# Short groups of small matrix products joined, and k turned by VectorE and DRAM for six units, in an HGRN2 + SwiGLU kernel

## The chip, the cores and the metric

The kernel runs on one core of a Trainium2 chip. The metric is the device time of one execution in microseconds (us). A core has engines that each work through their own instructions in order and wait for one another through semaphores: TensorE (PE, matrix products; PEld is its loading of weights), VectorE (DVE), ScalarE (ACT), GpSimd (POOL) and SyncE (SP, which here issues most of the transfers). SBUF is the on-chip memory with 128 partitions; PSUM is the memory that TensorE writes, in eight banks of 128 x 512 float32; DRAM lies outside the core.

## What is computed

Two blocks follow each other. The first is a linear attention with a gate, for 4 batches, 8 heads, 768 steps and heads 48 wide; the second is a SwiGLU layer on 3072 tokens of width 384, with a hidden width of 1536.

```python
f = 1.0 / (1.0 + np.exp(-f_logit))
for t in range(S):                       # S = 768, state is (B, H, 48, 48)
    state = f[:, :, t, :, None] * state + np.einsum('bhd,bhe->bhde', k[:, :, t], v[:, :, t])
    y[:, :, t] = np.einsum('bhd,bhde->bhe', q[:, :, t], state)
x = y.transpose(0, 2, 1, 3).reshape(B * S, H * D)
g = x @ w_gate
out = (g * (1 / (1 + np.exp(-g))) * (x @ w_val)) @ w_out
```

## The kernel before

The sequence is cut into 6 chunks of 128 steps. A *unit* is one batch b in one chunk c; units are numbered u = 4c + b, so there are 24. `attention(u)` (L527) is a generator: each `yield` ends a step, and the caller decides when the next one is written into the program. A unit's steps for c >= 2 (`SQUARES` = 2, L315), in their order:

- sigmoid of f on ScalarE (L541), transposes of f and k in 32 x 32 squares on VectorE (L547, L554), a backward scan of the gates (`tails`, L558), four tiny operations, k times tails (`kT`, L568: the decayed k), a forward scan (`head`, L571), the transpose of q (L574, after which `load_after` issues the next unit's loads), q times head (`qT`, L577), the state times the chunk's whole decay (`decayed`, L581);
- **scores**: 8 products kT by qT on TensorE into two PSUM banks (`sc`, L595); then four 128 x 128 transposes of kT on TensorE (L599), because the sum for the state needs k with time on the partitions (`kt`, copied to SBUF by ScalarE, L603);
- the causal mask of the scores on VectorE (`A`, two operations, L605), which empties the score banks;
- **output**: products of qT with the decayed state and of A with v (`y`, L623 and L627; for the last batch L648 with a block-diagonal state, whose buffer GpSimd clears, L585), two copies by ScalarE and ten small transfers that put y into `xT`;
- **the state's sum**: 8 products kt by v (`dS`, L668), added to `decayed` by VectorE (L675).

TensorE counts each float32 product twice in the profile: 8 products are x16 there, and 2 are x4.

Block c of the SwiGLU layer (`mlp_fifteen`, L848) takes the tokens of chunk c and runs while the units of chunk c+1 are worked on. `token_sums` (L856) forms sums of token tiles. Then come four *triples* (L883) of 15 products each (L896, PSUM tags A: 2 banks, B: 1, o: 2, and c, which shares the o banks; L1183). ScalarE copies the results out (L901: `aside` has three buffers), VectorE combines them (L795, L798), ScalarE applies SiLU (L912), VectorE multiplies (L846) into the hidden tiles `h`. After the triples `down_seven` (L976) runs 14 half pieces of the product with w_out (L999, L1062): one, six, two, three, four, five, seven. `hidden_sums` (L987) and two more rounds of differences prepare `h` for them, tile by tile.

The order of all this is written out by hand. A planner counts time in its own units (`PRODUCT` = 0.86 for one product, `DOWN` = 3.9 for one piece, L782) and writes a unit's next step into the program when its count reaches the due time in `UNITS_2` or `UNITS` (L785 to L789; `come_in`, L1201). VectorE operations handed to `lag` (L845) are written one piece later. At the end `in_order` (L1229) fixes the order of PE, DVE and ACT as written; POOL and SP are ordered by the scheduler. For each unit three times matter here: the scores, the output, and the state's sum right after the output. So TensorE leaves its large products twice per unit: once for scores and transposes, once for output and state's sum. PSUM banks for scores, y, kt and dS come from `bank` (L515), three banks in this stage.

At the very end each engine reads a flag (`values_load`, L1267) and branches past a slower path that is not taken here.

Of the kernel before, what the change touches and what calls it, by code (L numbers as in the profile page):

```python
# [9 lines left out]
FP32 = mybir.dt.float32  # L10
# [279 lines left out]
def short_path(ctx, tc, ident, least, judge, q, k, v, f_logit, moe_w_gate, moe_w_val, moe_w_out, out):  # L290
# [29 lines left out]
    ffn = ctx.enter_context(tc.tile_pool(name="ffn", bufs=2))  # L320
    sums_pool = ctx.enter_context(tc.tile_pool(name="sums", bufs=1))
# [205 lines left out]
    def attention(u):  # L527
# [4 lines left out]

        def transposed(name, src):
# [17 lines left out]
        qT = att.tile([128, HP, C], FP32, tag="qT", name="qT")  # L551
# [18 lines left out]
        head = att.tile([128, n], FP32, tag="head", name="head", bufs=1)  # L570
        nc.vector.tensor_tensor_scan(head, gate[:, 0:n], start, 1.0, op0=ALU.mult, op1=ALU.add)  # L571
# [5 lines left out]
        nc.vector.tensor_tensor(qT, qp, pairs(head)[:, :, 1:N1], ALU.mult)  # L577
        if 0 < c < SQUARES:
            load_after(u)
        if c:  # L580
            nc.vector.tensor_tensor(decayed[:, :, 0:D], states[b], whole.broadcast_to((128, HP, D)), ALU.mult)  # L581
        if c and b == B - 1:

            diagonal = att.tile([128, HP, 2 * D], FP32, tag="x", name="diagonal")
            nc.gpsimd.memset(diagonal, 0.0)  # L585
            for par in range(2):
                nc.scalar.copy(diagonal[rows_of(par), :, par * D:(par + 1) * D], decayed[rows_of(par), :, 0:D])
# [3 lines left out]
        sc = [bank("sc") for _ in range(2)]  # L591
# [4 lines left out]
        if c < NCH - 1:  # L596
            p = bank("kt")
            for a in range(HP):
                nc.tensor.transpose(p[:, a * C:(a + 1) * C], kT[:, a, :], ident)  # L599
        yield  # L600
        if c < NCH - 1:
            kt = att.tile([128, H, W], FP32, tag="kt", name="kt")
            nc.scalar.copy(kt, p.rearrange("t (h d) -> t h d", d=W))  # L603
        for par in range(2):
            nc.vector.tensor_tensor(A[:, par], sc[par].rearrange("p (a t) -> p a t", t=C),  # L605
                                    causal.unsqueeze(1).broadcast_to((128, HP, C)), ALU.mult)
        yield
# [57 lines left out]
        if c < NCH - 1:  # L665
            p = bank("dS")
            for h in range(H):
                nc.tensor.matmul(p[W * (h % 2):W * (h % 2) + W, (h // 2) * D:(h // 2 + 1) * D],  # L668
                                 lhsT=kt[:, h, :], rhs=v_[:, h, 0:D], start=True, stop=True)
            dS = p[:, 0:HP * D].rearrange("p (a d) -> p a d", d=D)  # L670
        yield
# [6 lines left out]
    def load_after(u):  # L678

        w = u + (1 if units[u][1] >= SQUARES else 2)  # L680
        if w < len(units) and (units[w][1] >= SQUARES) == (w == u + 1):
            load(w)

    def attention_steps(c):

        runs = [attention(c * B + b) for b in range(B)]
        parts = [3, 5, 2, 3]
# [23 lines left out]
    def hidden_tile():  # L711

        return ffn.tile([128, 4, TH], FP32, tag="h", name="h", bufs=NP)

    def mlp_plain(c):
# [9 lines left out]
        def part(j):  # L725
            if j % NP not in h:
                h[j % NP] = hidden_tile()
# [578 lines left out]
```

## Time and profile before

| | |
|---|---|
| median of 15 runs | 616.38 us (615.61 to 617.98) |
| the profiled execution | 616.81 us, its span 615.1 us |
| granted TensorE clock, mean | 0.996 of full speed |
| chunks 0 and 1 with the plain first block, 0 to 148 us | PE busy 140.1, DVE 130.4, ACT 63.5 us |
| block 2, 244.3 to 340.4 us (96.1) | PE 95.8, DVE 80.4, ACT 48.9 us |
| block 3, 340.4 to 436.5 us (96.1) | PE 95.8, DVE 80.4, ACT 48.9 us |
| block 4 with chunk 5, 436.5 to 529.4 us (92.9) | PE 92.4, DVE 73.3, ACT 44.8 us |
| block 5 without attention, 529.4 to 615.1 us (85.7) | PE 79.6, DVE 46.9, ACT 33.9 us |

Busy time is summed from the instructions' records on each engine. A matrix product's record overlaps the next one's, so the step from start to start is the better measure of what a product costs; the timeline gives starts. "Idle before, releaser" names how long an engine stood still before an instruction and who ended that wait.

### The profile page before, as it was taken

Reading aid. Unit: us, or ns where it says so; the run is one execution under the profiler, and the core shown is the slowest. Engines: PE = TensorE matmul, PEld = TensorE weight load, DVE = VectorE, ACT = ScalarE, POOL = GpSimd, SP = SyncE. Lnnn points to the kernel's source line nnn. Section 1 sums busy time; section 2 is a strip of 40 time slices with the busy share of each in tenths; the row PEclk is TensorE's granted clock in tenths of the full one; section 3 lists DMA queues with packets and bytes.
Section 4 is the critical chain, followed back from the end, with each engine's and each line's share of the span. In section 5 each row is a group of like instructions: output and inputs, shape, how many; then the busy total and the mean of one; then the engine's idle time right before and its main releaser. Section 6 shows DMA issues by size and latency. Waiting matters only on the chain.

```text
span 615.1 us, 10901 instructions
## 1 busy us (share of the span) xinstructions
PE 599.6 (97%) x4060; PEld 491.0 (80%) x4060; DVE 500.7 (81%) x961; ACT 291.4 (47%) x534; POOL 5.0 (1%) x27
## 2 busy tenths in 40 slices
PE   7799999999999999999999999999999999999996
PEld 4654545666888899888899888899988889988895
DVE  7899989878999988968997886987887985566741
ACT  2465645312766721557722567642267640366600
POOL 1000000000000000000000000000000000000000
PEclk9999999999999999999999999999999999999999
DMA  9999582005222334222124420323331300100001
GB/s 150 245 214 280 172 248 78 3 12 157 81 72 52 78 78 116 79 50 59 46 66 116 117 53 17 86 61 96 102 80 35 82 5 10 53 2 0 1 2 56
DMA packets 95679, 50.95 MB, mean 83 GB/s; under 512 B 56065, under 2 KB 89473, under 8 KB 95617
## 3 DMA queue, kind: packets, MB, share of 16 engines
q1 hardware_dynamic: 93600, 47.41, 31.5%
q10 hardware_dynamic: 2016, 2.75, 1.2%
q8 instruction: 34, 0.56, 0.4%
q14 instruction: 29, 0.23, 0.1%
HBM read 42.47 MB, written 4.72 MB: 77 GB/s over the span
## 4 chain that ended last, share of the span: by engine, by line
PE 93%; ACT 2%; DVE 1%; DMA 1%; issue 1%; ACTq 0%; DVEq 0%
PE o L999 19%; PE A L896 17%; PE B L896 13%; PE o L896 6%; PE gate L721 5%; PE o L746 5%; PE c L896 5%; PE val L721 5%; PE sc L595 4%; PE o L1062 3%; PE y L627 2%; PE y L648 2%; PE kt L599 2%; PE dS L668 2%; PE y L623 1%; DMA fraw<-in_f_logit_dram 1%
## 5 line engine op out<-in xcount | busy, mean ns | idle before, releaser
L896 PE MATMUL A<-xs,w_both 128*128 128x256 f32 x240 | 62.1, 381 | 1.1 <-ACT aside L901 1.1
L999 PE MATMUL o<-w_out,h 128*128 128x192 f32 x360 | 62.1, 327 | 0.2 <-ACT aside L901 0.2
L999 PEld LDWEIGHTS o<-w_out,h 128*128 128x128 f32 x360 | 58.6, 190 | 0.8 <-ACT aside L901 0.4
L795 DVE TENSOR_TENSOR c<-c,aside 128x512 f32<-128x512 f32 x60 | 41.0, 684 | 13.7 <-ACT aside L901 12.6
L896 PEld LDWEIGHTS A<-xs,w_both 128*128 128x128 f32 x240 | 44.8, 190 | 8.7 <-ACT aside L901 2.8
L901 ACT COPY c<-A 128x512 f32<-128x512 f32 x40 | 23.3, 583 | 58.2 <-PE A L896 51.2
L901 ACT COPY aside<-A 128x512 f32<-128x512 f32 x60 | 35.0, 583 | 33.6 <-PE A L896 33.6
L798 DVE TENSOR_TENSOR c<-c,aside 128x512 f32<-128x512 f32 x60 | 41.0, 684 | 7.3 <-ACT aside L901 7.3
L846 DVE TENSOR_TENSOR h<-h,c 128x256 f32<-128x256 f32 x100 | 41.0, 418 | 7.0 <-ACT h L912 6.7
L999 PE MATMUL o<-ws,h 128*128 128x192 f32 x240 | 41.7, 328 | 0.0
L896 PE MATMUL B<-xT,extra 128*128 128x256 f32 x160 | 41.4, 381 | 0.0
L896 PE MATMUL A<-xs,extra 128*128 128x256 f32 x160 | 41.2, 380 | 0.0
L896 PE MATMUL c<-xT,w_both 128*128 128x256 f32 x160 | 41.2, 380 | 0.0
L896 PE MATMUL B<-xs,w_both 128*128 128x256 f32 x160 | 41.1, 379 | 0.0
L912 ACT ACTIVATE h<-c 128x256 f32<-128x256 f32 x100 | 39.2, 415 | 2.8 <-DVE c L798 1.7
L901 ACT COPY aside<-B 128x512 f32<-128x512 f32 x60 | 34.9, 582 | 10.2 <-PE B L896 10.1
L999 PEld LDWEIGHTS o<-ws,h 128*128 128x128 f32 x240 | 39.2, 190 | 0.3 <-issue 0.2
L798 DVE TENSOR_TENSOR c<-o,c 128x512 f32<-128x512 f32 x40 | 27.4, 686 | 12.3 <-ACT h L912 9.5
L605 DVE TENSOR_TENSOR A<-sc,causal 128x512 f32<-128x512 f32 x48 | 30.6, 677 | 5.2 <-PE sc L595 5.2
L896 PEld LDWEIGHTS B<-xs,w_both 128*128 128x128 f32 x160 | 30.4, 190 | 4.1
L896 PEld LDWEIGHTS A<-xs,extra 128*128 128x128 f32 x160 | 30.3, 190 | 4.2
L896 PEld LDWEIGHTS c<-xT,w_both 128*128 128x128 f32 x160 | 30.3, 190 | 4.2
(135 smaller groups left out, 1154.2 us busy)
## 6 DMA issues: line engine op xcount, KB each, us to landing
fsquares<-in_f_logit_dram SPq DMA_DIRECT2D x64, 96.0 KB, 2.3
ksquares<-in_k_dram SPq DMA_DIRECT2D x64, 96.0 KB, 2.3
qsquares<-in_q_dram SPq DMA_DIRECT2D x64, 96.0 KB, 2.3
v<-in_v_dram SPq DMA_DIRECT2D x24, 192.0 KB, 3.5
w<-in_moe_w_gate_dram SPq DMA_DIRECT2D x6, 768.0 KB, 6.6
w<-in_moe_w_val_dram SPq DMA_DIRECT2D x6, 768.0 KB, 5.7
w<-in_moe_w_out_dram SPq DMA_DIRECT2D x6, 768.0 KB, 5.3
out_dram<-ob ACTq DMA_DIRECT2D x14, 192.0 KB, 2.9
```

What stands on the lines that cost most here:

```text
L595: nc.tensor.matmul(sc[par][:, a * C:(a + 1) * C], lhsT=kT[r, a, :], rhs=qT[r, a, :], start=True, stop=True)
L605: nc.vector.tensor_tensor(A[:, par], sc[par].rearrange("p (a t) -> p a t", t=C), causal.unsqueeze(1).broadcast_to((128, HP, C)), ALU.mult)
L721: nc.tensor.matmul(p, lhsT=w[:, j, i, :], rhs=xT[c][:, i, :], start=(i == 0), stop=(i == KT - 1))
L746: nc.tensor.matmul(p, lhsT=h[n // 2][:, n % 2 * 2 + b // 2, b % 2 * C:(b % 2 + 1) * C], rhs=w_out[:, j, :], start=(n == 0), stop=(n == NF ...
L795: nc.vector.tensor_tensor(dst, a, b, ALU.add)
L798: nc.vector.tensor_tensor(dst, a, b, ALU.subtract)
L846: lagging.append(lambda: f(*args))
L896: nc.tensor.matmul(p[name][:, n, :], lhsT=weights_of[a][:, n, j, :], rhs=tokens[b], start=fresh and n == 0, stop=True, skip_group_check=True)
L901: nc.scalar.copy(t, p[name])
L912: nc.scalar.activation(dst, src[:, 0, :], AF.Silu)
L999: nc.tensor.matmul(p[:, n, :], lhsT=lhsTs[j][:, n * C:(n + 1) * C], rhs=rhs[:, j, :], start=first and j == order[0] and n == 0, stop=j == ...
L1062: nc.tensor.matmul(p, lhsT=h[j][:, 2, n * C:(n + 1) * C], rhs=b22[:, j, :], start=j == order[0], stop=j == order[-1])
```

## The change

The program's arithmetic stays; its order and a few carriers change.

- Scores are due at one of four places per block, and a unit's output and state's sum are due just ahead of the next unit's scores (`times`). So y, dS and the next unit's sc stand next to each other on TensorE. In block 1 the joined groups are y0 dS0 sc1, y1 dS1 sc2, y2 dS2 sc3; in block 2 these three and y3 dS3 with the scores of chunk 4's first unit; in block 3 likewise four; in block 4 three without dS: 14 in all.
- Score banks: kind "b" as before, "o" from the o pair (7 units, at the ends of triples), "A" from the A pair (in the down pieces).
- For units 14 to 19 (`turned`) the TensorE transposes and ScalarE's copy go. VectorE transposes kT in 32 x 32 squares into the buffer of qT, SP writes it to DRAM in four transfers of 64 KB with runs of 128 B, and after the scores SP reads it back into kt in one transfer with runs of 2 KB. qT gets a second buffer. The transpose of q overwrites the same buffer, so it waits until the four transfers have read it.
- The forward scan writes over the gates; GpSimd clears their first column after each unit.
- `decayed` for c >= 2 moves behind the mask. v is loaded two units ahead, after dS, as a transfer of its own.
- `hidden_sums` and the two later rounds work on three tiles at once: 8 operations of 768 columns in place of 24 of 256 per block. Two token sums become one of 512 columns.
- `in_order` also fixes POOL and SP, so SP's flag read now stands ahead of the last two output transfers.

```diff
+        turned = (SQUARES + 1) * B + 1 < u < (NCH - 1) * B
+        if turned:
+            beside = qT.rearrange("p a t -> p (a t)").rearrange("p (i m) -> p i m", i=NI)
+            nc.vector.transpose(beside.rearrange("p i (a e) -> p a i e", e=Q), kT.rearrange("p a (i e) -> p a i e", e=Q))
+            turn = turn_pool.tile([Q, NI, HP, NI, Q], FP32, tag="turn", name="turn")
+            for r in range(NI):
+                nc.sync.dma_start(out=turn[:, :, :, r, :].rearrange("t i a e -> t (i a) e"),
+                                  in_=beside[Q * r:Q * (r + 1)].rearrange("t i (a e) -> t (i a) e", e=Q))
+        yield
+        nc.vector.tensor_tensor_scan(gate[:, 0:n], gate[:, 0:n], start, 1.0, op0=ALU.mult, op1=ALU.add)
...
-        nc.vector.tensor_tensor(qT, qp, pairs(head)[:, :, 1:N1], ALU.mult)
+        nc.vector.tensor_tensor(qT, qp, pairs(gate)[:, :, 1:N1], ALU.mult)
+        nc.gpsimd.memset(pairs(gate)[:, :, 0:1], 0.0)
...
-        sc = [bank("sc") for _ in range(2)]
+        sc = [score_bank(u) for _ in range(2)]
...
-        if c < NCH - 1:
+        if c < NCH - 1 and not turned:
             p = bank("kt")
             for a in range(HP):
                 nc.tensor.transpose(p[:, a * C:(a + 1) * C], kT[:, a, :], ident)
         yield
         if c < NCH - 1:
+            kt = att.tile([128, HP * C], FP32, tag="kt", name="kt")
+            if turned:
+                nc.sync.dma_start(out=kt, in_=turn.rearrange("t i a r e -> i t (a r e)"))
+            else:
+                nc.scalar.copy(kt, p)
...
+        if c >= SQUARES and u + 2 < len(units):
+            load(u + 2, "v")
...
+    STEPS = (-1.3, 0, 1.3, 2.8)
+    TRIPLE = PRODUCT * 15
+    def chain(k, q, qmul, turn=None, head=None):
+        return (*[k + t for t in STEPS], turn or k + 3.5, head or k + 3.5, q, qmul)
+    whole = NJ * TRIPLE + 7 * DOWN
+    between = [n * TRIPLE - 0.05 for n in range(NJ)]
+    down = [NJ * TRIPLE + n * DOWN / 2 - 0.05 for n in range(14)]
+    SCORES = {c: scores for c, scores in zip(range(2, NCH), (
+        ((12, "b"), (between[2], "o"), (down[2], "A"), (down[6], "A")),
+        ((PRODUCT - 0.05, "b"), (between[1], "o"), (between[3], "o"), (down[3], "A")),
+        *[((down[10] - whole, "A"), (between[1], "o"), (between[3], "o"), (down[3], "A"))] * (NCH - 4)))}
+    CHAINS = {c: chains for c, chains in zip(range(2, NCH), (
+        (chain(2.6, 4, 9), chain(14.5, 20, 23), chain(30, 37, 44), chain(57.4, 59, 61)),
+        (chain(-12, -8.5, -5), chain(3.5, 6, 9), chain(16, 28, 33, 21.5, 23.5), chain(40.1, 53, 55, 44.5, 52)),
+        *[(chain(-19.4, -11.2, -9.5), (-7.5, -6.3, 1.3, 2.2, 3.2, 5.5, 8, 10), chain(16, 28, 33, 21.5, 23.5), chain(40.1, 53, 55, 44.5, 52))] * (NCH - 4)))}
+    def times(c):
+        at = [t for t, _ in SCORES[c]]
+        outputs = [*at[1:], down[10] if c + 1 in SCORES and SCORES[c + 1][0][0] < -1 else LAST]
+        masks = {"b": 2, "o": 0.9, "A": 1.5}
+        return [[f, *steps, s + 0.02, s + masks[kind], s + 2.2, o, o + 0.01, o + 2.1]
+                for f, steps, (s, kind), o in zip(sigmoid, CHAINS[c], SCORES[c], outputs)]
+    def score_bank(u):
+        b, c = units[u]
+        kind = SCORES[c][b][1] if c >= SQUARES else "b"
+        if kind == "b":
+            return bank("sc")
+        return {"o": banks_o, "A": banks_a}[kind].tile([128, 512], FP32, tag=kind, name="sc")
-    DOWN_SUMS_AT = (22, 24, 26, 42)
+    DOWN_SUMS_AT = (28, 34, 38, 48)
...
+    def hidden_sums(odd):
+        a11, a21, a12, a22 = (h[odd][:, :, k, :] for k in range(4))
+        plus(s1[odd], a21, a22)
         minus(a21, a11, a21)
...
-    in_order(mark, (mybir.EngineType.PE, mybir.EngineType.DVE, mybir.EngineType.Activation))
+    in_order(mark, (mybir.EngineType.PE, mybir.EngineType.DVE, mybir.EngineType.Activation, mybir.EngineType.Pool, mybir.EngineType.SP))
```

## The prediction

> **What bounds the kernel.** I read the page's busy times first, then who ended TensorE's idle time in the stage that changes (148 to 529 us), then its timeline there, then VectorE's load by stage, and the queue of SP last.
>
> ```profile
> PE 599.6 (97%) x4060; PEld 491.0 (80%) x4060; DVE 500.7 (81%) x961; ACT 291.4 (47%) x534; POOL 5.0 (1%) x27
> ```
> ```profile
> PE A L896 <- ACT aside L901: 1.3, 5, 0.3
> PE o L999 <- ACT aside L901: 0.2, 1, 0.2
> ```
> ```profile
> 249.44 1.03 PE L896 MATMUL A<-xs,extra 128*128 128x256 f32 x4
> 250.40 1.16 PE L595 MATMUL sc<-qT,kT 48*128 48x128 f32 x16
> 251.49 0.66 PE L599 MATMUL kt<-idf,kT 128*128 128x128 f32 x4
> 251.98 1.03 PE L896 MATMUL B<-xs,extra 128*128 128x256 f32 x4
> 252.85 1.03 PE L896 MATMUL c<-xT,w_both 128*128 128x256 f32 x4
> ...
> 278.90 1.09 PE L627 MATMUL y<-A,v 128*64 128x128 f32 x16
> 279.82 0.62 PE L668 MATMUL dS<-v,kt 128*64 128x48 f32 x16
> 280.38 1.13 PE L896 MATMUL o<-xT,w_both 128*128 128x256 f32 x4
> 281.34 1.03 PE L896 MATMUL A<-xs,w_both 128*128 128x256 f32 x4
> ```
> ```profile
> 443.64 1.13 PE L896 MATMUL B<-xs,extra 128*128 128x256 f32 x4
> 444.61 1.03 PE L896 MATMUL c<-xT,w_both 128*128 128x256 f32 x4
> ```
> ```profile
> 148.00:244.30 96.30, 95.84 (x706) 84.82 (x705) 89.24 (x166) 51.43 (x96) 0.42 (x1) 1.00 0.32 85
> 244.30:340.40 96.10, 95.81 (x706) 85.11 (x705) 80.41 (x159) 48.86 (x93) 0.42 (x1) 1.00 0.28 75
> ```
> ```profile
> 383.04 1.86 SPq L638 DMA_DIRECT2D xT<-yT  x3
> ...
> 386.56 1.81 SPq L426 DMA_DIRECT2D ksquares<-in_k_dram  x4
> ```
> ```profile
> L1267 SPq TENSOR_LOAD <-flag x1: 517/517/517, 609.8 to 609.8; - x1
> ```
>
> TensorE is the bound: 97% busy, and in 381 us it waits for others only 1.5 us. So the end moves by what is taken off TensorE and by what new waits put on it; an operation on VectorE, ScalarE, GpSimd or SP costs nothing while it is in time. In the windows the columns are length, then busy time of PE, PEld, DVE and so on: VectorE is busy 89.2 of 96.3 us in block 1 and 80.4 of 96.1 in block 2, so it is the engine whose lateness could reach TensorE.
>
> **What the change takes off TensorE.** Starts give prices. Two products (x4) take 0.86 to 0.87 us (251.98 to 252.85). Ahead of the scores the step is 0.96 (249.44 to 250.40): entering a small group costs 0.10. After dS the first large product takes 0.96 (280.38 to 281.34): leaving costs 0.10. After the transposes it takes 0.87: nothing.
> - *Joining.* Output and state's sum, then at once the next scores: one entry and one exit less, 0.20. From dS to the scores I charge nothing beyond what dS to the large product costs. 14 joined groups: -2.8 us. Bounds: 0.10 each if that passage costs like an entry (-1.4), 0.20 (-2.8).
> - *Transposes.* They take 0.49 (251.49 to 251.98). Without them the scores are followed by a large product directly, and that costs the exit: 0.97 (443.64 to 444.61, a unit of chunk 5, which has no transposes), so 0.10 comes back. 6 x 0.39 = -2.3 us.
>
> The Trainium skill speaks against this second part: its page "VectorE: DVE Perf Modes", section "Rules for kernel authors", sends a 128 x 128 transpose to TensorE where PSUM will do as its target. Here PSUM did, and by that rule the transposes would stay and the sum below be -1.9 us instead of -4.2; the rows weigh otherwise, since the 0.49 us lies on the engine without slack.
>
> **What it adds, and what covers it.**
> - *VectorE* gets six transposes of kT at 1.1 us (as L554 and L574, 128 x 512), three in each of blocks 2 and 3. In turn, per block, 24 operations of 256 columns (start to start some 0.36: six h at 413.36 in 2.07 us, in pairs 0.40) become 8 of 768. No row has that shape; 512 columns take 0.68, 1152 take 1.36, in between about 0.95: 8.7 against 7.6, -1.1 us per block. Blocks 2 and 3 so go from 80.4 to 82.6 us of VectorE, under some 94 us of TensorE's products, which are the cover; without it each microsecond would show in full.
> - *GpSimd* clears 128 x 4 after each unit; its small clears take 0.1 to 0.2 us. The next gates' transpose on VectorE waits for it, but stands several operations later. Ahead of it in the same queue stands the clearing of `diagonal` (0.42 us), which waits for the transfers of y2; the next clear is due some ten planned units later. 0, with no bound above 0.5.
> - *SP.* A turned unit issues five transfers more: four writes and one read. An issue takes 0.43 to 0.62 us (four in 1.81, three in 1.86), so the writes take 1.8 to 2.5 us to issue. Landing: output transfers from SP take 1.9 to 3.3 us, v with its 1024 pieces of 192 B 3.5. A write here has 512 pieces of 128 B; I take 2.7 after the last issue, 4.5 us in all from the end of the transpose, bounds 3.7 (1.8 + 1.9) and 9.1 (2.5 + the 6.6 us of the 768 KB loads of weights). The read back stands in SP behind the v load, which waits for the previous dS; queued behind the read are the next unit's transfers. It is issued at the previous group and needed at the next one, at least 13 planned units later. 0.
>
> The skill's page "DMA: Bandwidth & Descriptors", section "Specifications", says that pieces under 512 B are handled by read-modify-write; it has no price for that, and if it brought the landing past the 8.4 us found below, the sum would be the slower rival's.
>
> *Where the writes can hurt.* VectorE cannot transpose q before the writes have read the shared buffer. The closest case is unit 17, in the first triple of block 3. I add VectorE's operations in their new order, each from its start to the next one's (256 columns 0.34, 512 columns 0.60, a transpose 0.95, a scan 1.15): token sums until 1.3 us after the block's first product, outputs 0.6, scan and tiny ones 1.5, kT 0.6, one combination 0.6, then the transpose of kT, which ends at 5.5 us. The transpose of q comes after three combinations and a scan, at 8.5. With 4.5 us it starts at 10.0: 1.5 late. Then 0.95, and nine operations, until the last o bank comes free at 14.0. TensorE gets there after 13.1 us of triple, 0.1 entry, 1.5 us of y and 0.56 of dS: 15.3. So 1.3 us of slack remain. Units 14 and 18 have 4.8 us before the transpose of q and 2.8 more before a bank is missed; 15 and 19 have 8.2; 16 has the down pieces between. 0 at my value.
>
> - *Block 1.* Weight sums for the down pieces (L798, 128 x 1152, 1.36 us each) move from planned time 22, 24, 26 into the third triple, where now also the masks, `decayed`, `hidden_sums` and the next unit's chain lie: 18.5 us of VectorE work (7.4 of the triple, 11.1 of the rest) against 13.1 of TensorE. At its end a copy of B waits for an `aside` buffer (0.4), and in the last triple a c product for its bank (0.7): +1.1. In turn one wait of before at 177.8 us (0.33 plus a restart of 0.10) falls away: -0.4. Together +0.7, bounds 0 and 2.
> - *The o banks.* Seven score groups use the pair that the next triple's third product needs 1.7 us later; the first mask (0.6) must have run by then. By the same adding VectorE arrives 0.4 to 2.6 us before the scores end. I charge 0.1 each, +0.7, like the small 0.03 to 0.1 us delays that the timeline shows at the ends of triples; bounds 0 and 3.5 (0.5 each).
> - *The end.* SP reads the flag (0.52 us) after the last output transfer, at 609.8. With SP in written order the read is 50 us earlier: -0.5, bounds -0.6 and 0.
>
> Sum: -2.8 - 2.3 + 0.7 + 0.7 - 0.5 = **-4.2 us** on the profiled execution (616.81, its span 615.1 and 1.7 around it), which lies 0.4 above the median. On the median, 616.4: **612.2 us**.
>
> **Rivals.**
> - *No new wait.* Block 1 and the o banks cost nothing: -2.8 - 2.3 - 0.5 = -5.6, **610.8**; the five waits for `aside` (1.3 us) could go too. For it: the walk above leaves 0.4 to 2.6 us everywhere but in block 1. Against: in block 1 18.5 us of VectorE's work meet 13.1; and four of those five come behind ScalarE's table load (L912) in a block's first triple, which stays where it was.
> - *The banks take it back.* All seven o groups wait 0.5 us and block 1 takes 1.4: -5.6 + 3.5 + 1.4 = -0.7, **615.7**. For it: 89 of 96 us on VectorE in block 1. Against: the kernel before lets VectorE run late without a wait (the last combination of block 1's third triple starts at 198.9, its product was through by 194.8).
> - *Slower: the writes land late.* One mechanism: SP's four writes in small pieces. At a landing L, unit 17 puts L - 5.8 on TensorE, units 14 and 18 L - 7.6 each; together these pass the gain of 4.2 at L = 8.4. At 9.1 they make 6.3, net +2.1: **618.5**. For it: nothing in this kernel writes DRAM in 128 B pieces. Against: v's 1024 small pieces land in 3.5.
> - That the change is not what it says (groups torn apart by the scheduler) gets no share: `in_order` fixes PE as written.
>
> **Numbers.** Forecast 0.55 (its own range 611.0 to 614.4), no new wait 0.20, banks 0.15, late writes 0.10. About 0.2%, 1.2 us, is what a measurement can tell from no change: faster means below 615.2. Forecast and first rival lie there, and a fifth of the third case: 0.77. Within: most of the banks' case, 0.12. Slower: 0.11. The range 610.2 to 616.6 leaves out the late writes and the tails.
>
> **What would show it.** On PE the scores right behind dS, 14 times, with the scores' first start some 0.15 us after the last of dS; the transposes into kt x56 instead of x80; the first large product after a joined group of a turned unit with a step of 0.97. PE's idle time at the large products 2 to 4 us, most of the new part between 180 and 210 us. VectorE's transpose of q waiting some 1.5 us for `turn`, once. Wrong if PE idles over 0.5 us ahead of scores in several groups, if the write's landing is above 6 us, or if dS to scores costs a second entry.

## The result, and the profile after

| | before | after |
|---|---|---|
| median | 616.66 us (615.61 to 617.99, 45 runs) | 614.73 us (614.10 to 615.21, 9 runs) |
| ratio after to before | | 0.9965, 95% interval 0.9957 to 0.9973 |
| the profiled execution, its span | 616.81, 615.1 us | 613.76, 612.0 us |

The change makes the kernel 1.9 us faster, less than half of the 4.2 us that were forecast. The line of busy times after the change:

```profile
PE 597.6 (98%) x4036; PEld 488.6 (80%) x4036; DVE 499.2 (82%) x882; ACT 285.3 (47%) x526; POOL 7.6 (1%) x51
```

TensorE has 24 products fewer (the six units' transposes) and VectorE 79 operations fewer. Where the time came from shows best from block to block. A block's length is measured here from the start of its first large product to that of the next block; block 5 runs to its last product.

| us | ahead of block 1 | block 1 | block 2 | block 3 | block 4 | block 5 | rest |
|---|---|---|---|---|---|---|---|
| before | 147.89 | 96.38 | 96.07 | 96.08 | 92.82 | 79.48 | 6.4 |
| after | 147.17 | 98.97 | 95.92 | 93.86 | 90.81 | 79.47 | 5.8 |
| difference | -0.7 | **+2.59** | -0.15 | -2.22 | -2.01 | 0.0 | -0.5 |

A unit's scores moved from block 3 into block 2 and another's from block 4 into block 3, so blocks 2 to 4 belong together: -4.38. These lengths are a better ruler than the whole time: over the sixteen profiles of the changed kernel and its variants an untouched block repeats within some 0.3 us and most within 0.02, while the start of block 1, ahead of everything that the variants reorder, lies anywhere between 147.17 and 149.11. The profiled pair's difference of 3.05 us holds 0.7 ahead of block 1, which is no more than that scatter. Without it 2.3 are left, near the medians' 1.9; blocks 1 to 5 alone make 1.8.

The waits of TensorE from 148 to 529 us after the change, in the columns of the waits shown before:

```profile
PE A L954 <- ACT aside L959: 1.2, 4, 0.3
PE B L954 <- ACT aside L959: 0.7, 1, 0.7
PE o L1053 <- DVE h L906: 0.5, 1, 0.5
PE c L954 <- DVE c L858: 0.5, 1, 0.5
PE o L1053 <- DVE A L628: 0.2, 1, 0.2
```

The first line was there before (1.3, and once more at the down pieces). The other four are new, one wait each, and all lie in block 1 (the last at 227 us, for the masks of the fourth unit, whose score bank the next piece needs). The timeline of block 1, where the brackets give the idle time and who ended it:

```profile
194.28 1.13 PE L954 MATMUL B<-xs,w_both 128*128 128x256 f32 x4 [0.74 <-ACT aside L959]
...
201.07 1.13 PE L954 MATMUL c<-xT,w_both 128*128 128x256 f32 x4 [0.48 <-DVE c L858]
...
210.62 1.57 PE L1053 MATMUL o<-w_out,h 128*128 128x192 f32 x8 [0.50 <-DVE h L906]
```

From start to start these steps are 0.91, 0.64 and 0.66 us longer than undisturbed ones, each followed by a restart of 0.10; that is more than the bracketed idle time, since modelled ends overlap. The step at 227 us is 0.35 longer, but not because VectorE is late: it stood still just ahead of these masks, for the scores.

```profile
226.93 1.29 DVE L628 TENSOR_TENSOR A<-sc,causal 128x512 f32<-128x512 f32 x2 [1.11 <-PE sc L615]
```

Now the engines in the third and fourth triple, after and before (length, then busy time of PE, PEld, DVE and ACT), and the small products that stood inside the third triple before the change:

```profile
179.43:207.36 27.93, 26.70 (x123) 22.39 (x122) 27.75 (x47) 18.00 (x36) 0.10 (x1) 1.00 0.23 56
```
```profile
178.73:208.94 30.21, 30.21 (x189) 25.30 (x187) 30.04 (x56) 21.01 (x40) 0.00 (x0) 1.00 0.32 79
```
```profile
181.41 1.16 PE L595 MATMUL sc<-qT,kT 48*128 48x128 f32 x16
...
183.00 1.03 PE L896 MATMUL A<-xs,w_both 128*128 128x256 f32 x4
...
190.00 0.67 PE L623 MATMUL y<-qT,decayed 48*64 48x128 f32 x16
...
192.07 1.13 PE L896 MATMUL c<-xT,w_both 128*128 128x256 f32 x4
```

VectorE is full in both. But before the change these two triples took TensorE 30.2 us, small products of two units among them, and VectorE kept up. After it the two waits of 0.91 and 0.64 us leave 26.4 us of TensorE's own work there, and VectorE has 27.8: TensorE has turned from the engine that VectorE keeps up with into one that waits for VectorE.

The other lines that answer to the prediction's are as it expected them. A joined group of a turned unit runs from output to scores without a large product between, and without transposes:

```profile
291.48 0.67 PE L649 MATMUL y<-qT,decayed 48*64 48x128 f32 x16
292.07 1.09 PE L653 MATMUL y<-A,v 128*64 128x128 f32 x16
293.00 0.62 PE L694 MATMUL dS<-v,kt 128*64 128x48 f32 x16
293.55 1.16 PE L615 MATMUL sc<-qT,kT 48*128 48x128 f32 x16
294.64 1.13 PE L954 MATMUL A<-xs,w_both 128*128 128x256 f32 x4
295.61 1.03 PE L954 MATMUL B<-xs,w_both 128*128 128x256 f32 x4
```

The scores begin 0.15 us after the last product of dS, and the first large product takes 0.97 from start to start. VectorE's transposes of kT (ns, least, median, most); the writes of the tile `turn`, who waited for it (us, times), the time from issue to landing; and the flag's read, now at 539.9:

```profile
L589 DVE STREAM_TRANSPOSE qT<-kT x6: 699/700/711, 276.5 to 396.2; 128x512 f32<-128x512 f32 x6
...
L592 SPq DMA_DIRECT2D turn<-qT x24: 582/626/627, 277.3 to 398.9; - x24
...
  DVE qT L599: 5.4, 3
...
DMA to landing us min/median/max: 2.1/2.4/5.0
```
```profile
L1321 SPq TENSOR_LOAD <-flag x1: 481/481/481, 539.9 to 539.9; - x1
```

### The profile page after: what moved, and what is told of

The parts are those of the page before. It is cut to its first block, busy times and chain, and to the rows that moved or that the text cites. A ratio compares the mean times of both kernels' runs of the same rounds, so it can differ in the third digit from the quotient of the medians.

```text
span 612.0 us, 10812 instructions
## 1 busy us (share of the span) xinstructions
PE 597.6 (98%) x4036; PEld 488.6 (80%) x4036; DVE 499.2 (82%) x882; ACT 285.3 (47%) x526; POOL 7.6 (1%) x51
## 4 chain that ended last, share of the span: by engine, by line
PE 74%; DVE 7%; ACT 4%; issue 2%; DMA 0%; SPq 0%; DVEq 0%; ACTq 0%
PE o L1053 19%; PE A L954 15%; PE B L954 12%; PE o L954 5%; PE o L775 5%; PE c L954 4%; PE sc L615 3%; PE o L1116 3%; PE y L653 2%; PE y L674 1%; PE y L649 1%; PE dS L694 1%; DVE c L858 1%; ACT L970 1%; PE kt L619 1%
## 5 line engine op out<-in xcount | busy, mean ns | idle before, releaser
L954 PEld LDWEIGHTS B<-xs,w_both 128*128 128x128 f32 x160 | 30.2, 190 | 5.2 <-ACT aside L959 1.1
L954 PEld LDWEIGHTS c<-xT,w_both 128*128 128x128 f32 x160 | 30.2, 190 | 5.1 <-DVE c L858 0.9
```

Source lines behind the costliest of these rows:

```text
L954: nc.tensor.matmul(p[name][:, n, :], lhsT=weights_of[a][:, n, j, :], rhs=tokens[b], start=fresh and n == 0, stop=True, skip_group_check=True)
```

## The experiments

Three theories for the 2.5 us that block 1 is longer than priced: **A**, the new place of the weight sums; **B**, the amount of VectorE's work against TensorE's in the triples; **C**, the coarse hidden sums. All kernels start from the changed one; each was timed beside the kernel before on its own chip, which the ratio refers to. Blocks are measured as in the table above; block 5 is 79.47 or 79.48 in all.

One wait blurs block 1. The fourth unit's output needs its block-diagonal state, whose buffer GpSimd clears only when the third unit's output transfers have landed. In the changed kernel ScalarE has copied that output by 225.8 us, but SP issues the transfers from 228.39 on, behind the next unit's loads. From the last piece ahead of it to the state's sum, this output takes 1.94 us where nothing waits. It takes 2.21 in the changed kernel, and 2.73, 2.57, 2.52 and 2.68 in e_sums_old, e_wout_late, e_no_turn and e_extra. The column "net" is block 1 less what goes beyond 1.94.

| kernel | block 1 | net | 2 | 3 | 4 | median, us | ratio to before, interval |
|---|---|---|---|---|---|---|---|
| after | 98.97 | 98.70 | 95.92 | 93.86 | 90.81 | 614.73 | 0.9965 (0.9957 to 0.9973) |
| e_sums_old | 99.17 | 98.38 | 95.93 | 93.85 | 90.81 | 615.19 | 0.9970 (0.9959 to 0.9981) |
| e_wout_late | 98.13 | 97.50 | 95.93 | 94.04 | 90.81 | 613.87 | 0.9948 (0.9934 to 0.9961) |
| e_output_early | 97.38 | 97.38 | 95.93 | 93.86 | 90.81 | 613.03 | 0.9939 (0.9926 to 0.9953) |
| e_no_turn | 99.29 | 98.71 | 97.10 | 95.30 | 90.81 | 617.25 | 1.0007 (0.9995 to 1.0018) |
| e_group_wout | 99.09 | 99.09 | 95.93 | 93.85 | 90.80 | 615.14 | 0.9975 (0.9965 to 0.9984) |
| e_apart | 98.64 | 98.64 | 96.45 | 94.37 | 91.48 | 616.76 | 0.9998 (0.9989 to 1.0007) |
| e_small_sums | 99.45 | 99.26 | 95.93 | 93.86 | 90.82 | 615.44 | 0.9981 (0.9971 to 0.9991) |
| e_early_wout | 96.57 | 96.57 | 95.92 | 93.85 | 90.80 | 612.46 | 0.9925 (0.9911 to 0.9938) |
| e_pool_sums | 102.44 | 102.44 | 95.92 | 93.86 | 90.81 | 618.31 | 1.0027 (1.0017 to 1.0037) |
| e_block1_old (computes something else) | 100.68 | 98.05 | 95.92 | 93.85 | 90.80 | 617.13 | 1.0005 (0.9995 to 1.0015) |
| e_best | 96.37 | 96.37 | 95.93 | 94.07 | 90.80 | 612.43 | 0.9929 (0.9915 to 0.9942) |
| e_block1_undo | 97.83 | 97.57 | 95.94 | 93.86 | 91.09 | 613.30 | 0.9950 (0.9936 to 0.9964) |
| e_extra (one run) | 100.73 | 99.99 | 95.93 | 93.87 | 90.82 | 616.91 | |
| e_undo_free_sp | 96.14 | 96.08 | 95.92 | 93.86 | 90.81 | 612.40 | 0.9927 (0.9914 to 0.9941) |

**The place of the sums.**

```diff
-    DOWN_SUMS_AT = (28, 34, 38, 48)
+    DOWN_SUMS_AT = (22, 24, 26, 42)
```

> The changed kernel with the weight sums of the down pieces back at planned times 22, 24, 26 and 42 (from 28, 34, 38, 48). In the changed kernel's profile block 1 (first product to first product of the next) is 98.97 us where 95.8 plus 0.7 was priced. Theory A (the place of the sums: in the third and fourth triple they hold up the combinations that free the buffers): the missing 2.5 us come back, block 1 about 96.5. Theory B (the amount: a joined group of 3.6 us left the triples of block 1, TensorE runs its 60 products with nothing between from 179 to 207 us, and VectorE's whole work up to the last combination, 57.4 us, is now longer than TensorE's 56.9; the order of that work does not matter): block 1 stays within 0.5 of 99.0. Theory C (the hidden sums, now 768 columns at once, stand ahead of combinations in the fourth triple): 99.0.

Block 1 took 99.17, net 98.38. The waits moved (the longest is now 1.03 us at an o bank in the third triple), and only some 0.3 us of the 2.5 came back. Theory A falls.

**One sum out of the stretch.**

```diff
-    DOWN_SUMS_AT = (28, 34, 38, 48)
+    DOWN_SUMS_AT = (28, 34, 63, 48)
```

> The changed kernel with one of the four weight sums, the one in place in w_out (1.41 us on VectorE at 199.0), moved from planned time 38 to 63, behind the triples and still ahead of the piece that reads it. Theory B: VectorE's work up to the last combination falls by 1.3 us and block 1 by as much, 98.97 to 97.7. Theory A: one of the three sums that stand in the third and fourth triple goes, about a third of 2.5, block 1 98.1. Theory C: the hidden sums stay, 99.0. Blocks 2 to 5 unchanged (95.9, 93.9, 90.8, 79.5).

98.13: 0.84 us less. As block lengths go this is theory A's number (98.1) and not B's (97.7), though A had fallen in the run before. Net of the fourth unit's wait it is 1.20 less, near the 1.3 that left VectorE. Against C, and for B once that wait is taken out.

**TensorE's output group back in the triples.**

```diff
         outputs = [*at[1:], down[10] if c + 1 in SCORES and SCORES[c + 1][0][0] < -1 else LAST]
+        if c == 2:
+            outputs[1] = between[3]
```

> The changed kernel with the output and the state's sum of the second unit in block 1 done ahead of the fourth triple, as before the change, not joined to the next scores in the down stage. Nothing leaves VectorE but two small operations come 0.7 us earlier. Theory B: TensorE gets 2.1 us of work (starts of y to the next product: 2.1) between the triples in which VectorE catches up; the waits at 193, 200 and 210 us (0.9, 0.6, 0.7 us by the waits of the profile) go, and the group torn apart costs 0.2: block 1 98.97 to 96.9. Theory A: the sums stay where they are; only the group's 0.2 is added if their place, not the pace, matters: 99.2. Theory C: in between, 98.

97.38, 1.59 us less (net 1.32) though the torn group costs TensorE more. The waits of 0.91 and 0.64 us are gone; the one ahead of the down pieces shrank from 0.66 to 0.40, and the step to the piece behind the fourth unit's scores, for its masks, grew from 0.46 to 0.86. Against A and for B, whose 96.9 lies nearer than C's 98, though B's number was missed. The same kernel ran a second time, under the label e_out_wout, for the scatter:

> A second look at the kernel with the second unit's output ahead of the fourth triple, on this chip: block lengths should repeat within 0.05 us (97.38, 95.93, 93.86, 90.81, 79.48).

97.36, 95.92, 93.85, 90.81, 79.47: here every block length repeats within 0.02.

**The transposes back on TensorE.**

```diff
-        turned = (SQUARES + 1) * B + 1 < u < (NCH - 1) * B
+        turned = False
```

> The changed kernel with all units' decayed k transposed by TensorE and copied by ScalarE, none by VectorE and DRAM; the rest as in the changed kernel. If the transposes were priced rightly (0.39 us each on TensorE), blocks 2 and 3 grow by 1.16 us each, 95.92 to 97.1 and 93.86 to 95.0, the whole by 2.3 us, to about 617.0 on a median of 614.7. Rival: the way by DRAM takes part of it back (VectorE's wait of 2.5 us for the writes, SP's queue), then each block grows by less than 0.7. Block 1, where no unit is turned, stays at 99.0.

Blocks 2 and 3 grow by 1.18 and 1.44 us, together 2.62. Block 3 holds one wait more, a step at 357.31 that is 0.31 us longer; e_block1_undo has the same wait in a block where nothing had been changed (block 4, 91.09 against 90.81). Without it the transposes are worth 2.3, what they were priced at, and the way by DRAM takes nothing of it back. Block 1 was to stay; it is 0.32 longer by the fourth unit's wait alone (net 98.71 against 98.70). With TensorE's transposes and the rest of the change the kernel does not differ measurably from the one before (ratio 1.0007).

**The whole third group back, with the sum late.**

```diff
-  ((12, "b"), (between[2], "o"), (down[2], "A"), (down[6], "A")),
+  ((12, "b"), (between[2], "o"), (between[3], "o"), (down[6], "A")),
-  (chain(2.6, 4, 9), chain(14.5, 20, 23), chain(30, 37, 44), chain(57.4, 59, 61)),
+  (chain(2.6, 4, 9), chain(14.5, 20, 23), chain(27.2, 32, 35.5), chain(57.4, 59, 61)),
-    DOWN_SUMS_AT = (28, 34, 38, 48)
+    DOWN_SUMS_AT = (28, 34, 63, 48)
```

> The changed kernel with the third joined group of block 1 (second unit's output, third unit's scores) ahead of the fourth triple in the o banks, not in the down stage; that unit's chain some 3 to 8 planned us earlier to fit; and the sum in place in w_out at 63 as in the run before. So far: moving the sums within the triples gave nothing (99.17), taking one of them out gave 0.84 (98.13), giving TensorE the output group there gave 1.59 (97.38). Theory B (amount of VectorE's work against TensorE's in the triples): TensorE gets 3.6 us more in the triples, VectorE 1.9 more (two masks, two small operations) and 1.3 less; the deficit is gone, block 1 is 95.8 to 96.3. Against it: the two masks now hold the o banks that the fourth triple's third product needs, behind a VectorE that is late; if that decides, 97 or more.

99.09: theory B's number fails. TensorE's longest step is now 1.81 us, in the down pieces, for the fourth unit's masks. VectorE's timeline of this kernel there:

```profile
224.74 1.35 DVE L858 TENSOR_TENSOR w_out<-w_out 128x1152 f32<-128x1152 f32 x1
226.01 1.82 DVE L858 TENSOR_TENSOR h<-h 128x768 f32<-128x768 f32 x2
227.74 1.28 DVE L628 TENSOR_TENSOR A<-sc,causal 128x512 f32<-128x512 f32 x2
```

The scores began at 225.20, and three operations stood ahead of their masks, the moved sum among them. So VectorE's debt does not end with the triples, as theory B had it; here it runs on to these masks, and work moved to a place short of them is not out of the stretch.

**The groups torn apart.**

```diff
+        outputs = [o if o == LAST else o - (PRODUCT if o < NJ * TRIPLE - 1 else DOWN / 2) for o in outputs]
```

> The changed kernel with all 14 joined groups torn apart: each output group one product (or half a down piece) ahead of the next unit's scores. Priced at 0.20 each: blocks 2 and 3 (four groups each) 95.92 to 96.7 and 93.86 to 94.7, block 4 (three) 90.81 to 91.4; the whole +2.8 less what block 1 does. If joining saves only the one entry (0.10), half of that. In block 1 three groups cost 0.6, and theory B gives nothing back since the group's work is no earlier by more than one product; 99.3 to 99.6.

Blocks 2 to 4 grow by 0.53, 0.51 and 0.67. Block 4's figure holds a new wait of 0.25 for an o bank with its restart of 0.10; without it 1.36 us for 11 groups, 0.12 each, not 0.20. In the down stage the starts show the 0.19 of an entry and an exit. At a triple's end the torn group costs only some 0.08: its exit falls on the triple's last product, which has a restart of 0.10 of its own in any case. Block 1, with three groups torn, was to take 99.3 to 99.6. It got 0.33 shorter (net 0.06): the second unit's output now comes half a piece sooner, and the wait of 0.66 us in the down pieces is gone.

**The hidden sums small again.**

```diff
-        pieces.insert(half + 12, (0, lambda: lag(hidden_sums, 0)))
+        for i, n in enumerate(range(0, NP, 2)):
+            pieces.insert(half + 10 + 3 * i, (0, lambda n=n: lag(hidden_sums, n)))
...
```

> The changed kernel with the hidden sums of each block as 24 operations of 256 columns, placed as before the change (those of even pairs every third product in the fourth triple), not as 8 of 768. Theory C (the large operations hold up the combinations behind them): block 1 from 98.97 to 98.0 or less. Theory B: VectorE gets 0.8 us more work for the whole block, of which 0.2 in the triples (six operations of 0.36 for two of 0.95): 98.9 to 99.3. Blocks 2 to 5 within 0.1 of 95.92, 93.86, 90.81, 79.47 by both.

99.45, longer by 0.48. Theory C falls; more work on VectorE, spread better, costs time: the step at the c bank, 0.64 us too long in the changed kernel, is 1.15 too long here. That is a little above B's 98.9 to 99.3.

**The early output and the sum behind the masks.**

```diff
+        if c == 2:
+            outputs[1] = between[3]
-    DOWN_SUMS_AT = (28, 34, 38, 48)
+    DOWN_SUMS_AT = (28, 34, 67, 48)
```

> The changed kernel with the second unit's output ahead of the fourth triple (block 1 was 97.38 so) and the sum in place in w_out at planned time 67, behind the fourth unit's masks, where VectorE was idle 2.0 us between 226 and 232 and 4.2 between 238 and 246. Theory B as it now stands: from 179 us to those masks at 226 VectorE has more to do than TensorE gives it time for; the order inside moves the waits only, and what leaves that stretch comes off the block. What waits the run with the early output still had: 0.50 us at the first down piece (h) and 0.75 at the masks. 1.3 us leave: block 1 96.1 to 96.3. If the waits came from single operations in bad places, not from the amount, one of the two stays: 96.6 to 97.0. In the run before last, with the sum at 63, just ahead of those masks, they were 1.8 us late and took the gain back.

96.57: the wait ahead of the down pieces is gone, 0.4 us at the masks stays. Of 1.3 us that left VectorE 0.81 came off the block. That misses theory B's 96.1 to 96.3 and stands at the edge of what the reading by single bad places asked for (one of the two waits stays, 96.6 to 97.0); this run does not tell the two apart. This kernel is faster than both of the case.

**The sums on GpSimd.**

```diff
+        def less(dst, a, b):
+            nc.gpsimd.tensor_tensor(dst, a, b, ALU.subtract)
-        return [lambda: minus(down_sums[1], b12, b11), lambda: minus(down_sums[2], b22, down_sums[1]),
-                lambda: minus(b12, b22, b12), lambda: minus(down_sums[4], b21, down_sums[2])]
+        return [lambda: less(down_sums[1], b12, b11), lambda: less(down_sums[2], b22, down_sums[1]),
+                lambda: less(b12, b22, b12), lambda: less(down_sums[4], b21, down_sums[2])]
-    DOWN_SUMS_AT = (28, 34, 38, 48)
+    DOWN_SUMS_AT = (10, 13, 24, 30)
```

> The changed kernel with all four weight sums of the down pieces on GpSimd, which is busy 1%, at planned times 10, 13, 24, 30; nothing else moved, the groups as in the changed kernel. VectorE loses 5.1 us in the first 60 us of block 1. Theory B: all its waits in block 1 go (0.91, 0.64, 0.66, 0.46 us, each with a restart of 0.10, and 0.27 at the diagonal copies): 98.97 to 95.8 or 96.1. If the group's move out of the triples costs by itself (banks, order on TensorE), VectorE's relief would leave half or more: 97.3 and up. Rival: GpSimd's operations are so slow, or slow VectorE's beside them so much, that the sixth sum piece at planned 55.5 waits: 99 or more. How long GpSimd takes for 128 x 1152 no run has shown; it has 25 us for the last two. Blocks 2 to 5 unchanged.

102.44: the rival holds. One of GpSimd's four operations in this kernel, then VectorE's beside it:

```profile
163.00 2.96 POOL L894 TENSOR_TENSOR ws<-w_out,ws 128x1152 f32<-128x1152 f32 x1
```
```profile
163.40 0.67 DVE L858 TENSOR_TENSOR c<-c,c 128x512 f32<-128x512 f32 x1
164.00 2.52 DVE L858 TENSOR_TENSOR c<-c,aside 128x512 f32<-128x512 f32 x1
```

A combination with `aside`, whose two operands lie in SBUF, takes 0.68 us alone; here it ends 0.6 us after GpSimd's operation does. The one just ahead of it takes one operand from PSUM (tag c) and runs its usual 0.67 us beside GpSimd. Four combinations were held so, by some 8.8 us in all (3.11, 2.52, 2.78 and 3.11 less four times 0.68), more than the 5.1 taken off VectorE. So the run does not test the relief it was meant for; by its sign it speaks for B.

**Block 1 in its old order, first try.** The scores also go back to the old banks.

```diff
+        if c == 2:
+            return [[k - 2.6, *chain(k, q, qmul), s, m, m, y, y, z] for k, q, qmul, s, m, y, z in (
+                (2.6, 4, 9, 12, 14, 17.3, 19), (12.5, 18.2, 24, 28, 30, 34.5, 36),
+                (28.5, 35, 41, 51.4, 52.5, 57, 58), (52, 57.1, 64, 68, 70, 72.5, 74))]
-    DOWN_SUMS_AT = (28, 34, 38, 48)
+    DOWN_SUMS_AT = (22, 24, 26, 42)
...
```

> The changed kernel with block 1 alone in the old order: its four units' chains, scores, outputs and weight sums at the planned times of the kernel before, no group joined there, scores in their old banks (TensorE's instructions of the block then stand in the order of the kernel before); the coarse hidden sums, the written order on GpSimd and SP and blocks 2 to 5 as changed. Theory B (the new order of block 1 takes its groups out of the triples and VectorE falls behind): block 1 as before the change, 96.4 against 98.97, so that joining three groups there cost 2.6 us instead of saving 0.6. Rival: something the whole kernel has changed (768 columns at once, the order of GpSimd and SP) is behind it: 98 or more. Blocks 2 to 4 stay at 95.92, 93.86, 90.81; whole about 612.2 on the median.

100.68, with waits of 1.35 and 2.36 us. It was no clean return: this kernel computes something else. `decayed` still stands behind the masks, and in the old order the second unit's (190.35 us) comes behind the third unit's `tails` (187.56), from which it takes the chunk's whole decay. (The expectation of the clean return below says it was the gates; the trace has the second unit's q multiplied at 178.69, before the third unit's gates are written at 184.75.) Nothing follows from this run.

**The last down piece's preparation behind the masks.**

```diff
                 nc.scalar.copy(kept["o", 0][:, :, 0:DH], kept["p"])
-                for odd in range(2):
-                    lag(minus, h[odd][:, :, 2, :], h[odd][:, :, 2, :], h[odd][:, :, 0, :])
...
                 lag(plus, kept["u"], kept["u"], kept["p"])
+                for odd in range(2):
+                    lag(minus, h[odd][:, :, 2, :], h[odd][:, :, 2, :], h[odd][:, :, 0, :])
```

> The last but one kernel (early output, sum in place at 67; block 1 was 96.57) with the two operations that prepare the last down piece (h minus h, 0.95 us each) moved behind the fourth unit's masks, one piece later, in all blocks. In block 1 they stood right ahead of these masks, and TensorE waited 0.4 us for them. Theory B: that wait goes, block 1 96.0 to 96.2. If VectorE's lateness there is of more than 1.8 us, part of the wait stays. Blocks 2 to 5 within 0.1 of 95.92, 93.86, 90.81, 79.47; the whole 0.4 us below the 612.46 of the run with the sum at 67.

Block 1 96.37, short of the 96.0 to 96.2 expected; the wait fell from 0.4 to 0.2 us, what is left when VectorE stands ready for these masks. Block 3 was 0.22 longer, which also happened (0.18) in e_wout_late, where nothing in it had been changed. The 0.4 us on the whole did not come: the median (612.43) cannot be told from that of the run with the sum at 67.

**Block 1 in its old order, clean.** The edits of the first try, and:

```diff
-        if c < SQUARES:
+        if c <= SQUARES:
             decay()
...
-        if c >= SQUARES:
+        if c > SQUARES:
             decay()
```

> A clean return of block 1 to the old order, after one that was none: there the third unit's gates, which share one buffer with the second unit's since the change, were written ahead of their last use, so the second unit's output was another, and the decayed state came after the masks, which held up the diagonal copies (waits of 1.35 and 2.36 us; 100.68). Here the decayed state stands with q's product as before the change, and so does the rest of TensorE's and VectorE's order. Theory B: block 1 96.4, as in the kernel before, 2.6 below the changed kernel's 98.97, the whole about 612.2. Theory D (the shared gates buffer or the coarse sums make any order of block 1 long): waits stay, 97.5 or more.

97.83, halfway, and as it stands theory D's number (97.5 or more). The two waits left (0.91 and 0.37 us) come through ScalarE. Its timeline in this kernel, then SP's:

```profile
181.51 1.28 ACT L555 ACT_TABLE_LOAD   x1 [1.94 <-DMA fsquares<-in_f_logit_dram]
```
```profile
169.54 6.74 SPq L664 DMA_DIRECT2D xT<-yT  x10
...
177.01 1.95 SPq L427 DMA_DIRECT2D fsquares<-in_f_logit_dram  x4
```

The sigmoid waits for f, whose loads stand behind ten output transfers on SP, and the copy of a product (L963, at 183.34) behind the sigmoid.

**One operation more on VectorE, in blocks 1 and 2.**

```diff
+    waiting += [(at, lambda: nc.vector.tensor_tensor(down_sums[1], down_sums[1], down_sums[1], ALU.max))
+                for at in (34.5, whole + 34.5)]
```

> The changed kernel with one more operation on VectorE, the larger of a weight sum and itself (128 x 1152, 1.35 us, which changes nothing), at planned time 34.5 of block 1 and again of block 2. Theory B: in block 1 VectorE has no time left, so the block grows by 0.8 to 1.35 us, 98.97 to 99.8 or 100.3; in block 2, with VectorE busy 85.1 of 95.9 us, it costs nothing: 95.92 to 96.1 at most. If waits come from single unlucky places and not from the amount, block 1 grows by less than 0.5 or block 2 by as much as block 1.

Blocks 1 and 2 of this kernel (length, then busy time of PE, PEld, DVE):

```profile
148.60:249.40 100.80, 97.02 (x706) 84.89 (x705) 90.31 (x152) 49.30 (x94) 0.94 (x6) 1.00 0.32 83
249.40:345.30 95.90, 95.61 (x714) 85.25 (x713) 85.90 (x151) 48.15 (x92) 0.84 (x5) 1.00 0.35 90
```

The same 1.35 us cost 1.76 in block 1 and 0.01 in block 2. 1.22 of it shows at one place, the step at the c bank (0.64 us too long becomes 1.86). Another 0.47 is the fourth unit's wait for its diagonal copies, which e_no_turn has without any added operation; net of it the cost is 1.29, inside the range expected. That is theory B at its plainest, though on one run: VectorE is the bound in block 1 and has slack in block 2.

**The old order, with SP free.** The edits of the clean return, and:

```diff
-    in_order(mark, (mybir.EngineType.PE, mybir.EngineType.DVE, mybir.EngineType.Activation, mybir.EngineType.Pool, mybir.EngineType.SP))
+    in_order(mark, (mybir.EngineType.PE, mybir.EngineType.DVE, mybir.EngineType.Activation))
```

> The clean return of block 1 to the old order (97.83 us), with SP and GpSimd no longer held to the written order in the last section. In that run two waits of TensorE (0.91 and 0.37 us, each with a restart of 0.10) hung on ScalarE's sigmoid of the third unit, which waited 1.94 us for its f: in the written order its loads stood on SP behind ten output transfers (issued in 6.7 us, and only then the f loads at 177.0), where the kernel before had issued them ahead, at 163.65. Theory B: with the loads ahead again block 1 is 96.4, that of the kernel before, and the whole 612.0 on the median. Against it: waits of another cause stay, 97 or more. The flag's read goes back behind the last output transfer, up to 0.5 us at the end.

SP's timeline again:

```profile
163.29 1.73 SPq L427 DMA_DIRECT2D fsquares<-in_f_logit_dram  x4
...
169.68 6.90 SPq L664 DMA_DIRECT2D xT<-yT  x10
```

The loads of f stand ahead of the output transfers, the waits are gone, and block 1 takes 96.14, less even than before the change. So the written order on SP cost the old block 1 1.69 us (GpSimd was freed with it, but the waits hung on SP's loads). Theory D falls: the shared gates and the coarse sums are still there. The new order of block 1 costs 98.97 - 96.14 = 2.83 us. SP's written order may have a part in that, the 0.27 us by which the fourth unit's output waits in the changed kernel. By the trace the other new waits there go back to VectorE or to the scores, and none to a load of f; the new order of block 1 with SP free was not run. The median, 612.40, cannot be told from those of the early output with the sum at 67 (612.46) and of the kernel after that (612.43); all three are faster than both kernels of the case, by some 0.7% and 0.4%.

## Why the prediction was right or wrong

- *Joining, -2.8.* Right in kind, a little large. Outside block 1 blocks 2 to 4 gained 4.38; taking the transposes back cost 2.62, or 2.3 without the one wait more. So joining and everything else made 1.8 to 2.1 for 11 groups, 0.16 to 0.19 each instead of 0.20. Tearing them apart by one product costs less, 0.12, for the reason told there. In block 1 joining gained nothing.
- *Transposes, -2.3.* Right: 2.3 to 2.6 when they are taken back. The rule of the Trainium skill that the prediction weighed (page "VectorE: DVE Perf Modes", section "Rules for kernel authors") would have kept them on TensorE; on this kernel, where TensorE is the bound, the runs decide against it.
- *VectorE in blocks 2 and 3, 0.* Right, and shown by e_extra for block 2. The load was not what was forecast: VectorE is busy 84.9 of 95.9 us in block 2 and 81.4 of 93.9 in block 3, where 82.6 each were given. Operations of 768 columns took 0.95, as interpolated. The transpose of kT took 0.70, not 1.1.
- *The writes, 0; wait of VectorE 1.5 us once.* The price was right, the wait was not: three waits, 5.4 us in all and 2.5 at most. None reached TensorE, which has no new wait in blocks 2 to 4. Landing was 2.4 us in the median and 5.0 at most, on top of some 2.5 us of issue. From the end of the transpose to the transpose of q unit 17 took 5.4 us, not 4.5, and unit 16 took 6.9; the slower rival needed 8.4.
- *The o banks, +0.7.* Too much: no wait appears ahead of an o product of a triple (the two o products that waited are in down pieces). So the measured 614.7 lies nearer to "The banks take it back" (615.7) than to the forecast by its number, but not by that sum.
- *The end, -0.5.* The read of the flag moved to 539.9 as predicted, and the profiled pair shows -0.55 from the start of VectorE's last operation on (6.01 to 5.46). But over the fourteen other profiles with SP in the written order that stretch is 5.4 to 6.2; the landing of the last output varies by as much as was gained.
- ***Block 1, "Together +0.7, bounds 0 and 2".*** This is the step that failed. Without the term the prediction's own prices put the block at 95.8 (96.38 less 0.20 for each of three groups), so it was 3.2 long. The mechanism was the one named, VectorE late behind the weight sums in the third and fourth triple, but its size was not worked out to the end. The text set 18.5 us of VectorE's work in one triple against 13.1 of TensorE's, and then charged two waits, 1.1 us less 0.4. The 5.4 us of debt were not followed further. Through the third and fourth triple VectorE is 27.75 of 27.93 us busy, so it pays nothing back there, nor, but for 0.48 us at 209.65, in the first down pieces; it stands still again at 225.8, for the fourth unit's scores. The h product in the down pieces waited too, and VectorE's three waits with their restarts make 2.5 us. Two waits for which the text charged nothing came on top: 0.45 at the fourth unit's masks, whose bank the next piece needs as soon as the scores are done, and 0.27 at the fourth unit's output. And the same joining that saved TensorE its entries took the cover away: before, a unit's scores with transposes (181.41 to 183.00) and another's output (190.00 to 192.07) gave VectorE 3.66 us inside the third triple, where now TensorE runs large products from 179.43 to 207.36. The runs: neither the order of the sums (net 98.38) nor their grain (net 99.26) brings back more than some 0.3 us, the amount does (net +1.29 for 1.35 us added, net -1.20 and -0.81 for 1.3 taken away), and so does TensorE's pace (net -1.32).

Put together, -4.2 with 2.5 more for block 1, 0.7 less for the o banks, 0.5 less for the end and 0.2 less gain from joining and transposes gives -1.7 us, beside the 1.9 measured. With block 1 in its old order and SP and GpSimd free again the kernel reaches 612.40, close to the 612.2 forecast; that is partly luck, since such a kernel has neither the three joined groups of block 1 nor the earlier read of the flag, for which the forecast counted 1.1 us.

What stays open: how low block 1 can get with its three groups joined, and with SP free. The prices say 95.8; the best joined or half-joined order tried gave 96.37.

## What to carry over

Where work is taken off the bounding engine, add up the next engine's work over the whole stretch until it is next idle, not over the stage where it is crowded; what it owes there is paid at the next places where the two meet, and rearranging only moves the place. Small work of the bounding engine can be another engine's cover: ask what it gave time to before it is moved away. An added operation that changes nothing, put once where an engine is thought to be full and once where it is thought to have slack, tells in one run which stage has which bound.

## What the runs showed of the hardware that was not expected

- An operation on GpSimd that reads two operands in SBUF holds up one on VectorE that also reads two there until it ends: 0.68 us became 2.52 to 3.11 us, four times out of four in e_pool_sums. One on VectorE with an operand in PSUM was not held (0.67 us at 163.40). The Trainium skill has this (page "SBUF — State Buffer", section "SBUF: two separate sides"): two of VectorE's and GpSimd's ports are one pair behind an exclusive lock, and an operation of VectorE with two inputs in SBUF is blocked for the whole length of one on GpSimd that reads SBUF. The rows agree.
- After a wait the first large product's step is 0.10 us longer (0.97 for two products, 194.28 to 195.25, in place of 0.87), and so it is at the last product of nearly every triple, where the trace names no wait. A second reason for a restart at the same place costs nothing more: in e_apart that last product stands behind an exit from a small group, and its step to the next group is 1.06 us, against 1.07 in the changed kernel.
- The transpose of kT into 32 x 32 squares took 0.70 us where those of k and q take 1.1. Its two sides differ in their strides from theirs; which stride it is was not tried.
